# Spectral mixing plus an MLP on one Trainium2 core: a step's rounding issued ahead of the next tile, step-2 copies together on ScalarE, and the last piece of w2 prepared later

## The chip, the core and the metric

The kernel runs on one core of one Trainium2 chip. The metric is the device time of one launch in microseconds. Three runs of the kernel before gave 1115.87, 1113.58 and 1115.8 us, a median of 1115.8 us. The profile is that of one more execution of the same program.

Five engines matter. TensorE (PE in the profile, its weight loads PEld) multiplies; VectorE (DVE) and ScalarE (ACT) work on tiles in SBUF and PSUM; GpSimd (POOL) folds inputs and scatters outputs; SyncE (SP) issues transfers. Each engine executes its own instructions in the order in which the program issues them, and waits in that order.

## The reference

For each of 8 batches, x is 3136 x 256. What is computed is the real part of a two-dimensional DFT followed by a normalised MLP with a residual:

```python
X = np.fft.fft(np.fft.fft(x, axis=1), axis=2)
x = X.real
mu  = x.mean(-1, keepdims=True)
var = ((x - mu) ** 2).mean(-1, keepdims=True)
xn  = (x - mu) / np.sqrt(var + 1e-6) * g_ln
out = x + np.maximum(xn @ w_ch1, 0.0) @ w_ch2        # 256 -> 1024 -> 256
```

The last axis of the DFT is never carried out for the MLP: the kernel multiplies it, with the gain and the mean's removal, into w1 beforehand. The input is real, so rows k and N-k of the spectrum share one computation: of 3136 rows in a batch 1569 are computed, and each gives two outputs ("plus" and "minus" side).

## The kernel before, in words

**Tiles.** The 8 x 1569 tokens stand in one row, cut into 49 chunks of 256 (the last has 264). A chunk's hidden layer is cut into 8 tiles of 128 of the 1024 features. One *step* s is one such tile: chunk s // 8, feature tile s % 8. There are 392 steps. Every operand of these products is split into a high part, rounded to TensorE's fast format, and a low part, the remainder; a product takes three passes (PASSES: w_hi with the low part, w_lo with the high part, w_hi with the high part).

**A step's three functions.** `moe1_a(s)` issues 6 matmuls into a PSUM tile `ab` (L364; two such buffers), then one copy of one half on ScalarE (`asb`, L368), then the sum and the difference of the halves on VectorE (`h`, L369 and L373). `moe1_b(s)` rounds that tile: ReLU with rounding on ScalarE (`h_hi`, L380), and the remainder on VectorE (`h_lo`, L381). `moe2(s)` issues 12 matmuls that multiply h_hi and h_lo of step s with w2 into PSUM tiles `acc` (L448). In the loop (L838) step s issues moe1_a(s), then the lists described below, moe1_b(s - 1), and moe2(s - 3).

**Side work.** Two dictionaries, `late` and `after`, hold functions by step number, written out before the loop. What is in `late[s]` is issued between moe1_a(s) and moe1_b(s - 1); what is in `after[s]` comes at the end of step s. The side work has a period of 8 steps. With s0 = 8c + 5 for chunk c:

- after s0: `step2(m, "mh")`, the second DFT step for the next tokens: 8 matmuls (L318) per m into one PSUM tile, and the copy `ckh` that rounds it (ScalarE, L336). There are 61 such m in the loop for 48 chunks, so some steps have two, the second of them in the PSUM tile with the tag "y". Then `residual` for both halves of chunk c: 8 matmuls `psy` (L467).
- late s0+1: `step2(m, "fl")`: the full copy `ck` (ScalarE, L338) and the remainder `ckl` (VectorE, L340), piece by piece where m's tokens lie in two chunks; then `residual_e` (ScalarE, L474 and L475, twice).
- late s0+2 and s0+3: `residual_y` (VectorE, L481, L482, L491, L492); the second time also L496 on VectorE and the square root `ve` on ScalarE (L498), which waits for it.
- late s0+4: `inverse_std`, four short VectorE instructions (L505 to L509).
- late s0+6 and s0+7: `finish` (VectorE, L521 and L523), and after it `store_out`: an indirect DMA on GpSimd's queue (L422) and plain DMAs on SP's.

The input side of the next batch (folding on GpSimd L227, L228, L233, L234, L245; `fold_hi` on ScalarE L239; `step1`, three long matmuls L282 and a copy on ScalarE L285) is spread over 24 steps of each batch, at most two pieces per chunk: step1 falls at s0+3 and s0+6, the GpSimd subtraction L245 at s0 and s0+3.

**Prologue.** Before the loop the weights are turned from 64-bit floats into pairs of tiles. For w2 this goes in four pieces of 512 columns: `convert_a` (VectorE L571, L573; ScalarE L579), `convert_b` (VectorE L584, L586), `finish_w2` (VectorE L637), `split_w2` (ScalarE L590, then GpSimd L591). Steps 0 to 5 are written out by hand between these pieces; the piece 3 of w2 is first needed by moe2(6), in step 9.

Of the kernel before, what the change touches and what calls it, by code (L numbers as in the profile page):

```python
# [144 lines left out]
def tile_kernel(ctx: ExitStack, tc: tile.TileContext, x, g_ln, w1, w2, tu, tab, tz, ty, tw, idx, out):  # L145
# [156 lines left out]
    def width(c):  # L302
        return LASTW if c == NCH - 1 else CW
# [4 lines left out]
    def step2(m, part, of=None):  # L308

        b, j = divmod(m, 8)  # L310
        base, end = gb[2 * j], gb[2 * j + 2]
        if "m" in part:
            ps2[m] = psum.tile([128, 2, CW], F32, tag="y" if m in second else "fft", name=f"ps2_{m}")
        ps = ps2[m]
        for g in (2 * j, 2 * j + 1) if "m" in part else ():
            k0, k1 = gb[g], gb[g + 1]
            for h in range(2):
                nc.tensor.matmul(ps[:, h, k0 - base:k1 - base], s2[b][:KP, g, 128 * h:128 * h + 128],  # L318
                                 tab_s[:, h, k0:k1], start=(h == 0 and g == 2 * j), stop=True,
                                 skip_group_check=True)  # L320
            if g == 0:
                nc.tensor.matmul(ps[:, 1, 0:50], zmu, tz_s, start=False, stop=True,
                                 skip_group_check=True)
        t = b * HALF + base
        stop = b * HALF + end
        while t < stop:
            c = min(t // CW, NCH - 1)
            n = min(stop, c * CW + width(c)) - t
            if c not in chunk:
                chunk[c] = (work.tile([128, 2, MAXW], F32, tag="ck", name=f"ck{c}", bufs=3),  # L330
                            work.tile([128, 2, MAXW], F32R, tag="ck_hi", name=f"ckh{c}", bufs=3),
                            work.tile([128, 2, MAXW], F32R, tag="ck_lo", name=f"ckl{c}", bufs=3))
            full, hi, lo = (x[:, :, t - c * CW:t - c * CW + n] for x in chunk[c])
            src = ps[:, :, t - b * HALF - base:t - b * HALF - base + n]
            if "h" in part and of in (None, c):
                nc.scalar.copy(hi, src)  # L336
            if "f" in part:
                nc.scalar.copy(full, src)  # L338
            if "l" in part and of in (None, c):
                nc.vector.tensor_tensor(out=lo, in0=src, in1=hi.bitcast(F32), op=ALU.subtract)  # L340
            t += n
# [4 lines left out]
    def hcols(c):  # L346

        return 2 * CW if width(c) == CW else LASTW + 32 + CW

    def moe1_a(s, passes=((0, 1), (1, 0), (0, 0))):  # L350
        c, f = divmod(s, 8)
        w = width(c)
        ch = chunk[c][1:]
        fs = slice(128 * f, 128 * f + 128)
        wt = (w1_hi, w1_lo)
        if w <= CW:
            ab = psum.tile([128, 2, CW], F32, tag="ab", name=f"ab{s}", bufs=2)
            pa, pb = ab[:, 0], ab[:, 1]
        else:
            pa = psum.tile([128, MAXW], F32, tag="ab", name=f"aa{s}", bufs=2)  # L360
            pb = psum.tile([128, MAXW], F32, tag="fft", name=f"bb{s}")
        for j, pt in ((0, pa), (1, pb)):
            for n, (wi, xi) in enumerate(passes):
                nc.tensor.matmul(pt, wt[wi][:, j, fs], ch[xi][:, j, :w],  # L364
                                 start=(n == 0), stop=(n == 2))
        asb = work.tile([128, MAXW], F32, tag="asb", name=f"asb{s}")
        h = hh[s] = work.tile([128, hcols(c)], F32, tag="h", name=f"h{s}", bufs=4)
        nc.scalar.copy(asb[:, :w], pa)  # L368
        nc.vector.tensor_tensor(out=h[:, :w], in0=asb[:, :w], in1=pb, op=ALU.add)  # L369
        if w > CW:  # L370
            nc.vector.tensor_tensor(out=h[:, w:w + 32], in0=asb[:, w - 32:w], in1=pb[:, w - 32:w],
                                    op=ALU.subtract)
        nc.vector.tensor_tensor(out=h[:, -CW:], in0=asb[:, :CW], in1=pb[:, :CW], op=ALU.subtract)  # L373

    def moe1_b(s):
        h = hh[s]
        n = hcols(s // 8)
        h_hi = work.tile([128, n], F32R, tag="h_hi", name=f"h_hi{s}", bufs=4)
        h_lo = work.tile([128, n], F32R, tag="h_lo", name=f"h_lo{s}", bufs=4)
        nc.scalar.activation(h_hi, h, AF.Relu)  # L380
        nc.vector.scalar_tensor_tensor(out=h_lo, in0=h, scalar=0.0, in1=h_hi.bitcast(F32),  # L381
                                       op0=ALU.max, op1=ALU.subtract)
        hh[s] = (h_hi, h_lo)

    def toks(c):
        t = [(0, 0), (128, 128)]
        if width(c) > CW:
            t.append((LASTW - 32, CW))
        return t
# [39 lines left out]
    def moe2(s, tiles=(0, 1, 2)):  # L429
        c, f = divmod(s, 8)  # L430
        hs = hh[s]
        ws = (w2_hi, w2_lo)
        for i, (t0, _) in enumerate(toks(c)):
            if i not in tiles:
                continue
            if f == 0:
                acc[c, i] = psum.tile([128, 2, D], F32, tag="y" if tail(i) else f"acc{c % 2}",
                                      name=f"acc{c}_{i}", bufs=1 if tail(i) else 2)
            if tail(i):
                for n, (wi, xi) in enumerate(PASSES):  # L440
                    nc.tensor.matmul(acc[c, i][:64, 0], hs[xi][:, t0:t0 + 64], ws[wi][:, f],
                                     start=(f == 0 and n == 0), stop=(f == 7 and n == 2),
                                     skip_group_check=True)
                continue
            for side in range(2):
                h0 = t0 + side * (hcols(c) - CW)
                for n, (wi, xi) in enumerate(PASSES):
                    nc.tensor.matmul(acc[c, i][:, side], hs[xi][:, h0:h0 + 128], ws[wi][:, f],  # L448
                                     start=(f == 0 and side == 0 and n == 0),
                                     stop=(f == 7 and n == 2), skip_group_check=True)  # L450
# [130 lines left out]
    def convert_b(key):  # L581
        high, e, f = conv[key]
        e = e.bitcast(I32)
        nc.vector.tensor_scalar(out=e, in0=e, scalar1=3, scalar2=0x7F800000,  # L584
                                op0=ALU.logical_shift_left, op1=ALU.bitwise_and)
        nc.vector.scalar_tensor_tensor(out=e, in0=high, scalar=-0x80000000, in1=e,  # L586
                                       op0=ALU.bitwise_and, op1=ALU.bitwise_or)

    def split(hi, lo, src, eng=nc.vector):
        nc.scalar.copy(hi, src)  # L590
        eng.tensor_tensor(out=lo, in0=src, in1=hi.bitcast(F32), op=ALU.subtract)  # L591
# [43 lines left out]
    def finish_w2(n):  # L635
        _, e, f = conv.pop(f"w2_{n}")
        nc.vector.scalar_tensor_tensor(out=f, in0=f, scalar=2.0 ** -20, in1=e, op0=ALU.mult,  # L637
                                       op1=ALU.mult)
        return f

    def split_w2(n, f):
        split(w2_hi[:, 2 * n:2 * n + 2], w2_lo[:, 2 * n:2 * n + 2],
              f.rearrange("p (f d) -> p f d", f=2), nc.gpsimd)

    after, late = {}, {}

    def add(s, fn, *args):

        after.setdefault(s, []).append((fn, args))

    def add_late(s, fn, *args):

        late.setdefault(s, []).append((fn, args))

    first = {}
    for m in range(3, 64):
        t0 = (m // 8) * HALF + gb[2 * (m % 8)]
        s = 8 * min(t0 // CW, NCH - 1) - 3
# [2 lines left out]
        first.setdefault(s, []).append(m)  # L661
    for s, ms in first.items():
        for m in ms:
            add(s, step2, m, "mh")
        for m in ms:
            add_late(s + 1, step2, m, "fl")
    for b in range(1, NB):
        need = 8 * (b * HALF // CW) - 3
        at = [need - d for d in ((45, 42, 37, 34, 29, 26, 21) if b > 1 else
# [15 lines left out]
    for c in range(NCH):  # L685
        n = len(toks(c))
        s = 8 * c + (5 if n == 2 else 4)
        if c == 0:
            s = 6
# [20 lines left out]
    with tc.manual_schedule(engines={E.PE, E.Activation, E.DVE, E.Pool}):  # L710
        with tc.manual_schedule(engines={E.SP}):
# [84 lines left out]
            f = finish_w2(0)  # L796
# [8 lines left out]
            f = finish_w2(1)  # L805
# [18 lines left out]
            f = finish_w2(2)  # L824
            split_w2(2, f)
            moe1_a(5)
            moe1_b(4)
            step2(2, "hfl")
            moe2(2)
            convert_a("w2_3", w2p[3])  # L830
            convert_b("w2_3")
            moe1_b(5)
            f = finish_w2(3)
            split_w2(3, f)

        main.append(True)
        lag, last = 3, 8 * NCH
        for s in range(6, last):  # L838
            moe1_a(s)
            for fn, args in late.get(s, ()):  # L840
                fn(*args)
            if s > 6:
                moe1_b(s - 1)
            moe2(s - lag)
            for fn, args in after.get(s, ()):
                fn(*args)
# [25 lines left out]
```

## Time and profile before

| what | value |
|---|---|
| median of three runs | 1115.8 us (1113.58 to 1115.87) |
| the profiled execution's own time | 1114.09 us |
| its span | 1112.2 us |
| PE busy | 1045.4 us, 94% |
| DVE busy | 857.3 us, 77% |
| ACT busy | 527.7 us, 47% |
| POOL busy | 355.8 us, 32% |
| mean granted clock of PE | 0.991 |

The span runs from the first to the last instruction; the run's time is 1.9 us more. Busy shares are of the span. PE's matmuls overlap: one takes about 0.28 us by the profile, and the next starts about 0.12 us after it did. A wait is listed as "who <- whom: us in total, times, longest". The chain of waits follows the work that ended last back through whatever released it.

### The profile page before, as it was taken

The page shows a single profiled execution, that of the slowest core. Times are in us where ns is not written, and L with a number is a line of the kernel's source. Part 1 is how long each engine was busy: PE and PEld are TensorE (multiplying, and loading weights), DVE is VectorE, ACT ScalarE, POOL GpSimd, SP SyncE. Part 2 cuts the span into 40 slices and gives each one's busy share as a digit, 9 for nine tenths or more (in the row PEclk, how much of TensorE's full clock was granted, in tenths as well). Part 3 has the DMA queues.
Part 4 walks back from the last instruction along what each step waited for, and adds up shares of the span by engine and source line. Part 5 has one row for each costly group of instructions (what it writes and reads, how often), then busy time and mean ns, then how long its engine had stood idle before and what let it go on. Part 6 is the DMA issues. An engine that isn't in the chain of part 4 may idle for free.

```text
span 1112.2 us, 22526 instructions
## 1 busy us (share of the span) xinstructions
PE 1045.4 (94%) x8313; PEld 1006.2 (90%) x8314; DVE 857.3 (77%) x2200; ACT 527.7 (47%) x1398; POOL 355.8 (32%) x456
## 2 busy tenths in 40 slices
PE   7889999999999999999999999999999999999997
PEld 5589999999999999999999999999999999989986
DVE  4788877877778868887787777887788778677685
ACT  2445544454455444554455445454455544444442
POOL 2427424530445224450263323541245301001001
PEclk9989999999999999999999999999999999999999
DMA  8931631153111810155011630127002131001001
GB/s 278 257 78 55 172 107 38 59 163 96 39 39 52 218 48 24 45 142 146 20 58 39 173 105 21 39 90 206 22 29 68 39 96 38 21 20 32 28 20 41
DMA packets 44612, 90.63 MB, mean 81 GB/s; under 512 B 6984, under 2 KB 33992, under 8 KB 43608
## 3 DMA queue, kind: packets, MB, share of 16 engines
q1 hardware_dynamic: 35335, 55.33, 17.3%
q0 software_dynamic: 8192, 32.82, 10.2%
q8 instruction: 66, 1.08, 0.4%
q10 hardware_dynamic: 976, 1.05, 0.3%
q14 instruction: 43, 0.34, 0.1%
HBM read 48.74 MB, written 40.44 MB: 80 GB/s over the span
## 4 chain that ended last, share of the span: by engine, by line
PE 46%; DVE 27%; issue 13%; ACT 10%; POOL 2%; DMA 1%; SPq 0%; POOLq 0%; ACTq 0%; DVEq 0%
PE acc L448 23%; PE ab L364 12%; DVE h_lo L381 8%; PE ps L318 4%; DVE h L369 4%; ACT h_hi L380 4%; DVE h L373 4%; PE psy L467 3%; DVE st L491 3%; ACT ye L475 2%; DVE ckl L340 2%; ACT asb L368 2%; PE ps L282 1%; DVE y L482 1%; DVE y L481 1%
## 5 line engine op out<-in xcount | busy, mean ns | idle before, releaser
L448 PE MATMUL acc<-w_hi,h_lo 128*128 128x256 f32 x1568 | 453.0, 289 | 40.0 <-DVE h_lo L381 39.9
L448 PE MATMUL acc<-w_lo,h_hi 128*128 128x256 f32 x1568 | 441.3, 281 | 0.7 <-POOL w_lo L591 0.7
L448 PE MATMUL acc<-w_hi,h_hi 128*128 128x256 f32 x1568 | 440.9, 281 | 0.0
L381 DVE SCALAR_TENSOR_TENSOR h_lo<-h,h_hi 128x512 fp32r<-128x512 f32 (+1 forms) x392 | 324.7, 829 | 88.9 <-ACT h_hi L380 88.9
L448 PEld LDWEIGHTS acc<-w_hi,h_lo 128*128 128x128 f32 x1568 | 296.4, 189 | 55.8 <-DVE h_lo L381 51.6
L448 PEld LDWEIGHTS acc<-w_lo,h_hi 128*128 128x128 f32 x1568 | 296.5, 189 | 0.9 <-POOL w_lo L591 0.9
L448 PEld LDWEIGHTS acc<-w_hi,h_hi 128*128 128x128 f32 x1568 | 296.3, 189 | 0.0
L422 POOL DMA_INDIRECT out<-o,idx_s x99 | 99.5, 1005 | 589.8 <-DVE o L521 581.6
L380 ACT ACTIVATE h_hi<-h 128x512 fp32r<-128x512 f32 (+1 forms) x392 | 248.5, 634 | 9.7 <-DVE h L373 9.1
L369 DVE TENSOR_TENSOR h<-asb,ab 128x256 f32<-128x256 f32 x384 | 159.4, 415 | 103.1 <-ACT asb L368 101.6
L368 ACT COPY asb<-ab 128x256 f32<-128x256 f32 x384 | 142.4, 371 | 202.2 <-PE ab L364 196.9
L364 PE MATMUL ab<-ckl,w_hi 128*128 128x256 f32 x768 | 221.5, 288 | 4.3 <-DVE h L373 4.3
L364 PE MATMUL ab<-ckh,w_lo 128*128 128x256 f32 x768 | 217.0, 283 | 0.3 <-ACT ckh L336 0.3
L364 PE MATMUL ab<-ckh,w_hi 128*128 128x256 f32 x768 | 216.1, 281 | 0.0
L373 DVE TENSOR_TENSOR h<-asb,ab 128x256 f32<-128x256 f32 x384 | 158.4, 413 | 0.0
L364 PEld LDWEIGHTS ab<-ckl,w_hi 128*128 128x128 f32 x768 | 146.1, 190 | 7.2 <-ACT ye L474 4.3
L364 PEld LDWEIGHTS ab<-ckh,w_lo 128*128 128x128 f32 x768 | 146.5, 191 | 2.8 <-ACT ckh L336 0.5
L364 PEld LDWEIGHTS ab<-ckh,w_hi 128*128 128x128 f32 x768 | 146.1, 190 | 0.0
L245 POOL TENSOR_TENSOR fl<-f,fh 128x512 fp32r<-128x512 f32 x49 | 63.1, 1288 | 106.0 <-ACT fh L239 105.3
L498 ACT ACTIVATE ve<-ve 128x2 f32<-128x2 f32 (+1 forms) x49 | 10.1, 206 | 173.5 <-DVE ve L496 173.5
L336 ACT CAST ckh<-ps 128x392 fp32r<-128x392 f32 (+49 forms) x112 | 34.4, 349 | 75.1 <-PE ps L318 72.8
L318 PE MATMUL ps<-tab_s,s 112*128 112x98 f32 (+1 forms) x512 | 65.6, 273 | 2.5 <-issue 2.5
(122 smaller groups left out, 1070.8 us busy)
## 6 DMA issues: line engine op xcount, KB each, us to landing
scratch<-s SPq DMA_DIRECT2D x49, 256.0 KB
s<-scratch SPq DMA_DIRECT2D x7, 1792.0 KB
x<-x SPq DMA_DIRECT2D x19, 448.0 KB
out<-o SPq DMA_DIRECT2D x154, 49.0 KB
w1p_all<-w SPq DMA_DIRECT2D x8, 512.0 KB
out<-o,idx_s POOLq DMA_INDIRECT x99, 3.8
x<-x POOLq DMA_DIRECT2D x3, 448.0 KB, 16.2
x<-x SPq DMA_DIRECT2D x6, 192.0 KB
```

Of the source, the lines that this page charges most:

```text
L245: nc.gpsimd.tensor_tensor(out=lo, in0=f, in1=hi.bitcast(F32), op=ALU.subtract)
L318: nc.tensor.matmul(ps[:, h, k0 - base:k1 - base], s2[b][:KP, g, 128 * h:128 * h + 128], tab_s[:, h, k0:k1], start=(h == 0 and g == 2 * j), ...
L336: nc.scalar.copy(hi, src)
L364: nc.tensor.matmul(pt, wt[wi][:, j, fs], ch[xi][:, j, :w], start=(n == 0), stop=(n == 2))
L368: nc.scalar.copy(asb[:, :w], pa)
L369: nc.vector.tensor_tensor(out=h[:, :w], in0=asb[:, :w], in1=pb, op=ALU.add)
L373: nc.vector.tensor_tensor(out=h[:, -CW:], in0=asb[:, :CW], in1=pb[:, :CW], op=ALU.subtract)
L380: nc.scalar.activation(h_hi, h, AF.Relu)
L381: nc.vector.scalar_tensor_tensor(out=h_lo, in0=h, scalar=0.0, in1=h_hi.bitcast(F32), op0=ALU.max, op1=ALU.subtract)
L422: stored(lambda: nc.gpsimd.indirect_dma_start(out, bass.IndirectOffsetOnAxis(ap=ix, axis=0), o, None), mybir.EngineType.Pool)
L448: nc.tensor.matmul(acc[c, i][:, side], hs[xi][:, h0:h0 + 128], ws[wi][:, f], start=(f == 0 and side == 0 and n == 0), stop=(f == 7 and n = ...
L467: nc.tensor.matmul(ps[:p, j, :129 + j], ck[:, j], ty_s[:, j, :129 + j], start=(j == 0), stop=True, skip_group_check=True)
```

## The change

Three edits.

In the loop, moe1_b(s - 1) is issued first in step s, ahead of moe1_a(s); before, it stood behind moe1_a(s) and behind `late[s]`. `moe1_b(5)`, which the prologue issued, is now the first instruction group of the loop.

Of step 2, the full copy `ck` (part "f") moves from the step after into the step that issues the matmuls and the rounding copy; in the step after only the remainder `ckl` (part "l") is left. The same is done for step2(2) in the prologue, where "hfl" becomes "hf" and then "l".

The end of w2's preparation (piece 3) leaves the prologue: `convert_b` goes to late[6], and `finish_w2` with `split_w2`, as the new function `make_w2`, to late[7].

```diff
+    def make_w2(n):
+        split_w2(n, finish_w2(n))
...
         for m in ms:
-            add(s, step2, m, "mh")
+            add(s, step2, m, "mhf")
         for m in ms:
-            add_late(s + 1, step2, m, "fl")
+            add_late(s + 1, step2, m, "l")
...
-            step2(2, "hfl")
+            step2(2, "hf")
+            step2(2, "l")
             moe2(2)
             convert_a("w2_3", w2p[3])
-            convert_b("w2_3")
-            moe1_b(5)
-            f = finish_w2(3)
-            split_w2(3, f)
+            add_late(6, convert_b, "w2_3")
+            add_late(7, make_w2, 3)
...
         for s in range(6, last):
+            moe1_b(s - 1)
             moe1_a(s)
             for fn, args in late.get(s, ()):
                 fn(*args)
-            if s > 6:
-                moe1_b(s - 1)
             moe2(s - lag)
```

## The prediction

> **What bounds the kernel now.** I read the page first, then PE's waits inside the loop, then the waits of DVE and ACT, and then one period of eight steps in the chain and in the timelines. Page and PE's waits (60 to 1100 us):
>
> ```profile
> PE 1045.4 (94%) x8313; PEld 1006.2 (90%) x8314; DVE 857.3 (77%) x2200; ACT 527.7 (47%) x1398; POOL 355.8 (32%) x456
> ...
> L381 DVE SCALAR_TENSOR_TENSOR h_lo<-h,h_hi 128x512 fp32r<-128x512 f32 (+1 forms) x392 | 324.7, 829 | 88.9 <-ACT h_hi L380 88.9
> ...
> L245 POOL TENSOR_TENSOR fl<-f,fh 128x512 fp32r<-128x512 f32 x49 | 63.1, 1288 | 106.0 <-ACT fh L239 105.3
> ```
>
> ```profile
> PE acc L448 <- DVE h_lo L381: 38.3, 54, 1.0
> PE ab L364 <- DVE h L373: 4.1, 1, 4.1
> ```
>
> PE is the bound, and what it loses in the loop is one thing: moe2 waits for h_lo, 54 times, about once per chunk. Such a wait costs more than its idle time. This is one of them, in PE's timeline, and the chain around it:
>
> ```profile
> 337.06 0.28 PE L364 MATMUL ab<-ckh,w_hi 128*128 128x256 f32 x1
> 338.13 0.38 PE L448 MATMUL acc<-w_hi,h_lo 128*128 128x256 f32 x1 [0.78 <-DVE h_lo L381]
> 338.35 0.27 PE L448 MATMUL acc<-w_lo,h_hi 128*128 128x256 f32 x1
> ```
>
> ```profile
> 322.03 0.71 PE ab L364 x6
> 322.74 1.44 PE acc L448 x12
> 324.18 1.76 PE ps L318 x16
> 325.94 0.92 PE psy L467 x8
> 326.86 0.73 PE ab L364 x6
> ```
>
> Matmuls otherwise start 0.12 us apart. Start to start across the wait is 1.07 us, and 0.22 to the one behind it: 0.95 + 0.10 = 1.05 lost, 0.26 more than the idle 0.78. So 38.3 + 54 x 0.26 = **52 us** hang on h_lo. A step of PE is 0.70 to 0.71 + 1.43 to 1.44 = 2.14 us; step 2 with two m adds 1.76 (0.88 each), the residual 0.92.
>
> Why h_lo is late shows in DVE's timeline of that period (s0 = step of the 1.76 us), with ACT's:
>
> ```profile
> 329.94 0.46 DVE L340 TENSOR_TENSOR ckl<-ps,ckh 128x286 fp32r<-128x286 f32 x1 [0.47 <-ACT ck L338]
> 331.38 0.69 DVE L381 SCALAR_TENSOR_TENSOR h_lo<-h,h_hi 128x512 fp32r<-128x512 f32 x1 [0.98 <-ACT h_hi L380]
> 331.99 0.41 DVE L369 TENSOR_TENSOR h<-asb,ab 128x256 f32<-128x256 f32 x1
> 332.32 0.41 DVE L373 TENSOR_TENSOR h<-asb,ab 128x256 f32<-128x256 f32 x1
> 332.65 0.28 DVE L481 TENSOR_TENSOR y<-ye,psy 128x129 f32<-128x129 f32 x1
> ...
> 333.72 0.83 DVE L381 SCALAR_TENSOR_TENSOR h_lo<-h,h_hi 128x512 fp32r<-128x512 f32 x1
> ...
> 335.14 0.28 DVE L481 TENSOR_TENSOR y<-ye,psy 128x129 f32<-128x129 f32 x1
> ...
> 337.38 0.69 DVE L381 SCALAR_TENSOR_TENSOR h_lo<-h,h_hi 128x512 fp32r<-128x512 f32 x1 [0.79 <-ACT h_hi L380]
> ```
>
> ```profile
> 325.08 0.49 ACT L336 CAST ckh<-ps 128x392 fp32r<-128x392 f32 x1 [1.34 <-PE ps L318]
> ...
> 336.73 0.62 ACT L380 ACTIVATE h_hi<-h 128x512 fp32r<-128x512 f32 x1
> ```
>
> These h_lo belong to s0, s0+1 and s0+2. After PE's burst (step 2, residual) DVE first does h(s0+1) and the remainders, in alternation with ACT's copies, then h_lo(s0), which has waited since h(s0); every later h_lo stands behind the next tile's h and a residual. PE wants h_lo(s0+2) at 337.35 and gets it at 338.13.
>
> **The change part by part.** *Order in a step.* No instruction is added or removed. Before: h(s), late(s), h_lo(s-1). After: h_lo(s-1), h(s), late(s). Queued behind the waiting h_hi(s-1) on ACT is now asb(s), and behind h_lo(s-1) on DVE is h(s), for which PE waits two steps on, since `ab` has two buffers. So a ring appears: h_hi, h_lo, h, h, next h_hi. Its length: h_hi start to h_lo start 336.73 to 337.38 = 0.65; h_lo to h 331.38 to 331.99 = 0.61; then 0.33, then 0.41 and a hand-over, which I estimate at 0.04: **2.04 us**, under PE's 2.14. Late DVE work runs while h_hi does, so it lengthens the ring only beyond 0.70: first residual 332.65 to 333.72 = 1.07, step 0.61 + 0.66 + 1.07 = 2.34; second residual with the square root 335.14 to 337.38 = 2.24, step 3.51; remainders of two m up to about 1.0, step 2.3; inverse_std and finish about 0.7 and 0.8 (finish from L521 to the next h_lo, below: 0.78), step 2.06 at most. Eight steps: 2.04 x 3 + 2.1 + 2.34 + 3.51 + 2.06 x 2 = **18.2 us** on DVE. PE's eight: 8 x 2.14 + 61/48 x 0.88 + 0.92 = 19.2, so on average PE stays the bound.
>
> ```profile
> 321.78 0.48 DVE L521 SCALAR_TENSOR_TENSOR o<-acc,r,y 128x256 f32<-128x256 f32 x1
> 322.17 0.47 DVE L523 SCALAR_TENSOR_TENSOR o<-acc,r,y 128x256 f32<-128x256 f32 x1
> 322.56 0.69 DVE L381 SCALAR_TENSOR_TENSOR h_lo<-h,h_hi 128x512 fp32r<-128x512 f32 x1
> ```
>
> Locally I walk the same period. ACT rounds and copies the two m behind PE's 325.94 until about 327.0, then h_hi(s0) to 327.65, just as moe1_a(s0+1) ends at 327.59; h_lo(s0) to 328.3, h(s0+1) to 329.0, 1.4 after its matmuls. Remainders and h_lo(s0+1) follow, h(s0+2) at 331.0 to 331.4. First residual: h(s0+3) 0.2 later still against PE, 1.7. Second: h(s0+4) 3.51 - 2.14 = 1.4 later, **3.1 us** behind its matmuls. h_lo(s0+2) ends near 333, 4 us before PE wants it: that wait goes wholly. The one that is late next is `ab`: moe1_a(s+2) starts 30 matmuls of 0.118 after the end of moe1_a(s), less 0.28 for the modelled end, plus 0.12, so h(s) may be 3.3 us late. The margin at s0+4 is 0.2 us; where a step1 falls at s0+3, PE's extra 0.7 makes it 0.9.
>
> What eats that margin is GpSimd. DVE's and POOL's timelines:
>
> ```profile
> 323.91 2.83 DVE L381 SCALAR_TENSOR_TENSOR h_lo<-h,h_hi 128x512 fp32r<-128x512 f32 x1
> ```
>
> ```profile
> 323.54 1.29 POOL L245 TENSOR_TENSOR fl<-f,fh 128x512 fp32r<-128x512 f32 x1
> 324.77 0.73 POOL L233 TENSOR_TENSOR f<-zw 128x256 f32<-128x256 f32 x1
> 325.46 0.73 POOL L234 TENSOR_TENSOR f<-zw 128x256 f32<-128x256 f32 x1
> ```
>
> An h_lo that starts inside the folding takes 2.83 instead of 0.69. All of that, (829 - 690) ns x 392 = 54 us, lies today where DVE would wait for PE's burst anyway; in the ring it delays h. 54 us over the 49 foldings (L245) is 1.1 each; they fall on some 25 chunks, in which step1 lengthens PE by 1.4 and the slack to 19.2 + 1.4 - 18.2 = 2.4, 58 us in all. The average is covered, single hits are not. I put the remaining `ab` waits at 0.25 us a chunk, between 0 (the walk as it stands) and 0.75 (margin overrun by 0.5, with the 0.26): **+12 us**, bounds 0 and +36.
>
> The Trainium skill, "SBUF — State Buffer", section "Who interferes with whom", says that a DVE instruction with two SBUF inputs and a GpSimd one that reads SBUF exclude each other for the whole of whichever starts first. The trace agrees, but its 2.14 us of blocking spans three POOL instructions; by the page's one (1.29) the 49 foldings could take at most 63 us, and the slower rival below would shrink to about 1076.
>
> *Copies in one go.* ACT's and DVE's waits:
>
> ```profile
> ACT ck L338 <- DVE ckl L340: 41.0, 46, 0.9
> DVE ckl L340 <- ACT ck L338: 18.5, 47, 0.5
> ```
>
> Both waits go. They stand in the same stretch ahead of the late h_lo, so their worth is inside the 52, not beside it. `ck` now runs in ACT's wait for PE's burst; without that cover it would put its 0.5 us on h_hi(s0).
>
> *w2's end.* Chain, DVE, PE and POOL at the loop's start:
>
> ```profile
> 70.95 2.56 PE acc L448 x12
> ```
>
> ```profile
> 65.12 0.42 DVE L584 TENSOR_SCALAR ew<-ew 128x512 int32<-128x512 int32 x1
> 65.57 0.69 DVE L586 SCALAR_TENSOR_TENSOR ew<-w1p_all,ew 128x512 int32<-128x512 int32 x1
> 66.18 0.69 DVE L381 SCALAR_TENSOR_TENSOR h_lo<-h,h_hi 128x512 fp32r<-128x512 f32 x1
> 66.78 0.69 DVE L637 SCALAR_TENSOR_TENSOR fw<-fw,ew 128x512 f32<-128x512 f32 x1
> 68.42 0.42 DVE L369 TENSOR_TENSOR h<-asb,ab 128x256 f32<-128x256 f32 x1 [0.96 <-ACT asb L368]
> ```
>
> ```profile
> 69.32 0.55 PE L364 MATMUL ab<-ckl,w_hi 128*128 128x256 f32 x1 [4.08 <-DVE h L373]
> ```
>
> ```profile
> 68.20 1.27 POOL L591 TENSOR_TENSOR w_lo<-fw,w_hi 128x512 fp32r<-128x512 f32 x1 [5.85 <-ACT w_hi L590]
> ```
>
> h(6) stands behind convert_b (65.12 to 66.18) and, through ACT's copy of w2, behind fw; PE waits 4.08 us for it and then runs at half pace (2.56 for 1.43; the matmuls of both steps behind the wait lose some 2 us). After the change h_lo(5) starts 1.06 earlier and another 0.5 for the copies of step2(2), near 64.6, and h(6), next in the queue, runs from 65.2 to 65.9, 3.3 us ahead of today's 69.2. Given back: DVE then has convert_b 1.06, h_lo(6) 0.6, h(7) 0.66 and fw 0.6 to 68.8, ACT some 0.6, POOL 1.27: w_lo at 70.7. PE is at moe2(6) near 69.0 (65.9 + 0.71 + 1.43, a wait for h(7) until 68.2, 0.71) and waits 1.7; I allow 0.6 for what DVE's later steps lose. Net 3.3 + 2 - 1.7 - 0.6 = **-3 us**, from 0 (the half pace comes back at the new wait) to -5 (no loss in the later steps, w_lo in time).
>
> Sum from the execution's 1114.1: - 52 + 12 - 3 = **1071 us**. That execution lies 1.7 under the median and inside the runs' spread, so I add nothing.
>
> **The rivals.** *Nothing is left over* (the margin always holds): 1114 - 52 - 5 = 1057. For it: the walk. Against it: the margin of 0.2. *The wait moves to `ab` nearly in full*: 0.75 a chunk, +36: 1114 - 52 + 36 - 3 = 1095. For it: hand-overs of 0.1 more in three ring steps use up the margin. *The reorder doesn't reach the stall*, because the square root still holds h_hi back (0.79 idle stays): 1113. Against it: h_lo(s0+2) has 4 us to spare. *Slower*: every folding blocks a ring h_lo for the full 2.14: 49 x 2.14 = 105 against 58 of slack, 47 us: 1114 - 52 + 12 - 3 + 47 = 1118. It decides from (52 - 12 + 3 + 58) / 49 = 2.06 us per folding; the average today is 1.1.
>
> **How the numbers follow.** Forecast (1062 to 1085) 0.55, nothing left 0.12, wait moved 0.20, no effect 0.05, slower 0.08. Three runs spread over 0.2%, so less than that counts as the same: faster 0.87, same 0.05, slower 0.08. 1058 to 1096 leaves the last two and a little at the low end outside.
>
> **What would show it.** Right: PE's waits for h_lo fall from 54 to a few, none near 1 us; the waits between ck and ckl vanish; a wait of `ab` on h appears with some 5 to 20 us in total, at s0+4; the 4.08 us at the loop's start become under 2 and a wait for w_lo appears; DVE waits more for h_hi (88.9 us now) since the ring exposes it. Wrong: waits for h_lo stay near 38 us, or `ab` on h passes 40 us with long h_lo next to POOL's folding.

## The result and the profile after

The changed kernel takes 1058.2 us (median of four runs, 1057.27 to 1058.92) against 1115.8 us on the same chip: a ratio of 0.9485, with a 95% interval of 0.9466 to 0.9503. That is 57.6 us less. The forecast was 1071, the range 1058 to 1096; the time lies at the range's lower edge, where the rival "nothing is left over" (1057) stood.

The page after the change, engines and the groups that answer to those shown before (columns: busy us, mean ns of one, idle before and what ended it):

```profile
PE 1027.1 (97%) x8314; PEld 999.4 (95%) x8314; DVE 824.7 (78%) x2200; ACT 533.9 (51%) x1398; POOL 364.7 (35%) x456
...
L448 PE MATMUL acc<-w_hi,h_lo 128*128 128x256 f32 x1568 | 441.3, 281 | 1.1 <-DVE h_lo L381 0.9
...
L381 DVE SCALAR_TENSOR_TENSOR h_lo<-h,h_hi 128x512 fp32r<-128x512 f32 (+1 forms) x392 | 295.4, 754 | 182.9 <-ACT h_hi L380 180.1
```

PE's waits after the change, 60 to 1100 us (us in total, times, longest):

```profile
PE ab L364 <- DVE ve L505: 2.6, 2, 1.5
PE pse L257 <- DVE ckl L340: 2.3, 2, 1.2
...
PE ab L364 <- DVE h L373: 1.2, 2, 0.7
...
PE acc L448 <- POOL w_lo L591: 1.0, 1, 1.0
PE acc L448 <- DVE h_lo L381: 0.7, 1, 0.7
```

The wait for h_lo, 38.3 us in 54 times before, is one wait of 0.7, and that one stands at 1045 us, behind the loop; inside the loop there is none. The waits between ck and ckl are gone. DVE waits twice as long for h_hi as before (180 us against 88.9): the ring is there, and it costs nothing, since PE doesn't wait for it. Engines by stretch, before and after (length of the window, then busy us of PE, PEld, DVE, ACT and POOL, PE's granted clock, the DMAs' share and GB/s):

```profile
200.00:300.00 100.00, 95.53 (x779) 93.14 (x778) 78.45 (x210) 49.24 (x132) 29.68 (x39) 1.00 0.31 89
900.00:1000.00 100.00, 94.59 (x781) 92.43 (x781) 73.70 (x207) 45.06 (x125) 11.17 (x20) 1.00 0.14 42
```

```profile
200.00:300.00 100.00, 99.85 (x834) 98.84 (x833) 80.17 (x217) 52.56 (x141) 36.34 (x44) 1.00 0.33 94
900.00:1000.00 100.00, 100.00 (x854) 100.00 (x854) 80.31 (x225) 51.38 (x140) 11.14 (x22) 1.00 0.10 31
```

PE is busy throughout at full clock: inside the loop hardly any wait is left to be won.

The period that the prediction walked through comes 8.95 us earlier now (its residual starts at 316.82 instead of 325.77). ACT and DVE in it:

```profile
316.12 0.49 ACT L336 CAST ckh<-ps 128x392 fp32r<-128x392 f32 x1 [1.25 <-PE ps L318]
316.51 0.49 ACT L338 COPY ck<-ps 128x392 f32<-128x392 f32 x1
...
317.59 0.43 ACT L338 COPY ck<-ps 128x286 f32<-128x286 f32 x1
317.88 0.67 ACT L380 ACTIVATE h_hi<-h 128x512 fp32r<-128x512 f32 x1
```

```profile
318.58 0.98 DVE L381 SCALAR_TENSOR_TENSOR h_lo<-h,h_hi 128x512 fp32r<-128x512 f32 x1 [2.45 <-ACT h_hi L380]
319.48 0.41 DVE L369 TENSOR_TENSOR h<-asb,ab 128x256 f32<-128x256 f32 x1
319.81 0.41 DVE L373 TENSOR_TENSOR h<-asb,ab 128x256 f32<-128x256 f32 x1
320.14 1.09 DVE L340 TENSOR_TENSOR ckl<-ps,ckh 128x392 fp32r<-128x392 f32 x3
321.16 0.68 DVE L381 SCALAR_TENSOR_TENSOR h_lo<-h,h_hi 128x512 fp32r<-128x512 f32 x1
...
322.09 0.41 DVE L373 TENSOR_TENSOR h<-asb,ab 128x256 f32<-128x256 f32 x1
...
329.65 0.69 DVE L381 SCALAR_TENSOR_TENSOR h_lo<-h,h_hi 128x512 fp32r<-128x512 f32 x1
...
331.70 0.69 DVE L381 SCALAR_TENSOR_TENSOR h_lo<-h,h_hi 128x512 fp32r<-128x512 f32 x1 [0.70 <-ACT h_hi L380]
```

All copies of step 2 are on ACT in one go behind PE's burst; the remainders (three, L340) follow without a pause. h(s0+1) ends at 320.2 and h(s0+2) at 322.5; the walk, moved by 8.95, had 320.1 and 322.5. Two h_lo of steps without long late work are 329.65 to 331.70 = 2.05 us apart; the ring was put at 2.04.

**A landmark inside the loop.** The first residual starts anywhere between 61.0 and 68.0 us in the traces of this study: the prologue ahead of it, in which hardly any of the edits acts, takes longer in one execution than in another. So beside whole times I compare the stretch from the fourth residual (chunk 3) to that of chunk 47, both starts in PE's timeline, here before and after:

```profile
131.37 1.08 PE L467 MATMUL psy<-ty_s,ck 128*128 128x129 f32 x8
1070.55 1.08 PE L467 MATMUL psy<-ty_s,ck 128*128 128x129 f32 x8
```

```profile
132.93 1.08 PE L467 MATMUL psy<-ty_s,ck 128*128 128x129 f32 x8
1015.30 1.08 PE L467 MATMUL psy<-ty_s,ck 128*128 128x129 f32 x8
```

939.2 us before, 882.4 after: 56.8 us, practically the whole gain, lie there. Some 1.5 us of it are no work of the change: in the execution before, PE ran at about half its clock (granted clock 0.51) from 179.8 to 183.3 us; that of the kernel with w2's edit alone, where it didn't, takes 937.7 us for the same stretch.

### The profile page after: what moved, and what is told of

Read it like the earlier page. It is cut to its first block, busy times and chain, and to the rows that moved or that the text cites. A ratio compares the mean times of both kernels' runs of the same rounds, so it can differ in the third digit from the quotient of the medians.

```text
span 1056.3 us, 22463 instructions
## 1 busy us (share of the span) xinstructions
PE 1027.1 (97%) x8314; PEld 999.4 (95%) x8314; DVE 824.7 (78%) x2200; ACT 533.9 (51%) x1398; POOL 364.7 (35%) x456
## 4 chain that ended last, share of the span: by engine, by line
PE 56%; DVE 19%; issue 14%; ACT 7%; POOL 2%; DMA 1%; SPq 0%; POOLq 0%; DVEq 0%; ACTq 0%
PE acc L448 30%; PE ab L364 16%; DVE h_lo L381 7%; PE ps L318 4%; ACT h_hi L380 4%; DVE h L369 3%; DVE h L373 3%; PE psy L467 2%; PE ps L282 2%; DVE st L491 1%; POOL out L422 1%; DMA x<-x 1%; ACT ckh L336 1%; ACT s L285 1%; PE ps L275 1%
## 5 line engine op out<-in xcount | busy, mean ns | idle before, releaser
L448 PE MATMUL acc<-w_hi,h_lo 128*128 128x256 f32 x1568 | 441.3, 281 | 1.1 <-DVE h_lo L381 0.9
L381 DVE SCALAR_TENSOR_TENSOR h_lo<-h,h_hi 128x512 fp32r<-128x512 f32 (+1 forms) x392 | 295.4, 754 | 182.9 <-ACT h_hi L380 180.1
L422 POOL DMA_INDIRECT out<-o,idx_s x99 | 102.4, 1034 | 580.5 <-DVE o L521 572.3
L364 PE MATMUL ab<-ckl,w_hi 128*128 128x256 f32 x768 | 222.1, 289 | 5.5 <-DVE ve L505 2.6
L364 PE MATMUL ab<-ckh,w_lo 128*128 128x256 f32 x768 | 215.8, 281 | 0.3 <-ACT ckh L336 0.3
L364 PE MATMUL ab<-ckh,w_hi 128*128 128x256 f32 x768 | 215.1, 280 | 0.0
L373 DVE TENSOR_TENSOR h<-asb,ab 128x256 f32<-128x256 f32 x384 | 158.1, 412 | 0.0
L364 PEld LDWEIGHTS ab<-ckl,w_hi 128*128 128x128 f32 x768 | 144.5, 188 | 11.1 <-issue 7.0
L368 ACT COPY asb<-ab 128x256 f32<-128x256 f32 x384 | 138.6, 361 | 18.2 <-PE ab L364 15.6
L364 PEld LDWEIGHTS ab<-ckh,w_lo 128*128 128x128 f32 x768 | 145.0, 189 | 2.8 <-ACT ckh L336 0.5
L364 PEld LDWEIGHTS ab<-ckh,w_hi 128*128 128x128 f32 x768 | 144.8, 188 | 0.0
L245 POOL TENSOR_TENSOR fl<-f,fh 128x512 fp32r<-128x512 f32 x49 | 63.5, 1295 | 46.7 <-ACT fh L239 45.9
L336 ACT CAST ckh<-ps 128x392 fp32r<-128x392 f32 (+49 forms) x112 | 39.5, 355 | 54.6 <-PE ps L318 33.0
```

The lines of the kernel that those rows point to most:

```text
L245: nc.gpsimd.tensor_tensor(out=lo, in0=f, in1=hi.bitcast(F32), op=ALU.subtract)
L364: nc.tensor.matmul(pt, wt[wi][:, j, fs], ch[xi][:, j, :w], start=(n == 0), stop=(n == 2))
L422: stored(lambda: nc.gpsimd.indirect_dma_start(out, bass.IndirectOffsetOnAxis(ap=ix, axis=0), o, None), mybir.EngineType.Pool)
```

## The experiments

### One part at a time

The three edits were made alone, and the first two together.

```diff
 # the order alone
+            if s > 6:
+                moe1_b(s - 1)
             moe1_a(s)
             for fn, args in late.get(s, ()):
                 fn(*args)
-            if s > 6:
-                moe1_b(s - 1)
```

> The kernel before with only the loop's order changed (moe1_b(s-1) first). Theory: the order alone takes the wait of moe2 for h_lo away, whatever the copies do: that wait under 3 us in PE's list, time 50 to 56 us under the kernel before; the alternation of ck and ckl is still there (some 40 and 18 us) and now delays h(s0+2), so a wait of ab on h of 0 to 5 us is left. Rival (the parts add up): the copies carry a good part, the order alone gives only 25 to 40 us.

1106.9 us, ratio 0.9907 (0.9892 to 0.9922); the stretch 929.6, of which some 3 are lost at half clock near 184 and 822 us. Only 9 us: theory and rival both fall. PE's waits (60 to 1045 us; up to 1100 it is 38.0 us in 43 times), ACT's, and one place in DVE's and PE's timelines:

```profile
PE ab L364 <- DVE ve L505: 37.3, 42, 1.4
```

```profile
ACT ck L338 <- DVE ckl L340: 45.8, 46, 1.7
```

```profile
936.54 0.41 DVE L369 TENSOR_TENSOR h<-asb,ab 128x256 f32<-128x256 f32 x1
936.87 0.41 DVE L373 TENSOR_TENSOR h<-asb,ab 128x256 f32<-128x256 f32 x1
```

```profile
937.43 0.36 PE L364 MATMUL ab<-ckl,w_hi 128*128 128x256 f32 x1 [0.68 <-DVE ve L505]
```

The wait for h_lo has gone, and one of the same size has come for `ab`, once a chunk. The listing names L505, the instruction started last; what PE's buffer needs is h(s0+4), which ends at 936.87 + 0.41 = 937.28, 0.15 before PE starts. The alternation of ck and ckl now stands ahead of h(s0+2): by the ends of L364 and L373 in 41 chunks, h(s0+2) is done 2.7 us behind its matmuls instead of 1.5 in the changed kernel, and h(s0+4) 4.2 instead of 3.1.

```diff
 # the copies alone
-            add(s, step2, m, "mh")
+            add(s, step2, m, "mhf")
-            add_late(s + 1, step2, m, "fl")
+            add_late(s + 1, step2, m, "l")
-            step2(2, "hfl")
+            step2(2, "hf")
+            step2(2, "l")
```

> The kernel before with only step 2's copies together on ACT. Theory: they shorten the queue ahead of the late h_lo by 1.3 to 1.8 us per chunk (walked through the same period: h_lo(s0) from 331.4 to about 329.8, h_lo(s0+2) from 337.4 to about 335.6, wanted by PE near 336.8), which is more than the wait of about 1.05 us; so this edit alone too takes 35 to 52 us, and the two edits overlap almost fully. Rival, the prediction as it was written would allow it: the copies' waits are cover only, the edit alone gives under 15 us.

1059.9 us, ratio 0.9495 (0.9478 to 0.9512); the stretch 885.4. PE's waits (60 to 1100 us):

```profile
PE ab L364 <- DVE h L373: 3.2, 1, 3.2
PE acc L448 <- DVE h_lo L381: 2.6, 5, 1.4
```

The copies alone bring nearly everything (56 us; the theory had 35 to 52).

```diff
 # w2's end alone
-            convert_b("w2_3")
             moe1_b(5)
-            f = finish_w2(3)
-            split_w2(3, f)
+            add_late(6, convert_b, "w2_3")
+            add_late(7, make_w2, 3)
```

> The kernel before with only the end of w2 spread (convert_b in late[6], finish and split in late[7]; moe1_b(5) stays where it was). Theory: the 4.08 us wait of ab near 65 us falls under 2.5 us and the half pace behind it goes, a wait for w_lo of 0 to 2 us appears: 2 to 5 us less in all. Rival: what is won at 69 us is given back at steps 7 to 9, no change (within 2 us).

1114.2 us, ratio 0.9977 (0.9966 to 0.9989): 2.1 us, at the foot of the theory's range. PE at the loop's start:

```profile
70.91 0.36 PE L364 MATMUL ab<-ckl,w_hi 128*128 128x256 f32 x1 [0.85 <-DVE h L373]
75.69 0.39 PE L448 MATMUL acc<-w_hi,h_lo 128*128 128x256 f32 x1 [1.72 <-DVE h_lo L381]
81.60 0.35 PE L448 MATMUL acc<-w_hi,h_lo 128*128 128x256 f32 x1 [1.13 <-DVE h_lo L381]
```

The 4.08 became 0.85; two waits for h_lo follow, the given-back part (the expected wait for w_lo doesn't show here).

The order and the copies together, without w2's edit:

> The changed kernel without the spreading of w2. Theory: order and copies together give 53 to 57 us under the kernel before, the 4.08 us wait near 65 us shrinks to 1 to 3 us because h(6) no longer stands behind late work, so w2's spreading is worth 0 to 3 us. Rival: the wait stays at 4 us with the half pace behind it, and this is 5 or more us slower than the changed kernel.

1057.9 us, ratio 0.9476 (0.9461 to 0.9490), 58.5 us less where the theory had 53 to 57; the stretch 882.2. The loop's start in PE's timeline, and the chain there:

```profile
67.90 0.55 PE L364 MATMUL ab<-ckl,w_hi 128*128 128x256 f32 x1 [3.26 <-DVE h L373]
```

```profile
69.52 2.17 PE acc L448 x12
71.69 0.70 PE ab L364 x6
```

A wait of 3.26 us stays, with some of the half pace behind it (2.17 for 1.43). The wait is between theory and rival, and yet the whole time is that of the changed kernel. Between the first and the fourth residual this kernel takes 68.4 us, the changed one 68.2 and, in a second execution, 67.2.

So the parts don't add up: 9 (order) + 56 (copies) + 2 (w2) would be 67. Either of the first two moves work out of one and the same queue. The order alone puts h_lo ahead and h behind, and the wait moves; only the shorter queue takes it away.

### Which half of the copies' edit

Here all of ck is copied, then all of ckl computed, but still in the step after:

```diff
-            add_late(s + 1, step2, m, "fl")
+            add_late(s + 1, step2, m, "f")
+        for m in ms:
+            add_late(s + 1, step2, m, "l")
```

> The kernel before, but in the step after step 2 all of ck is copied first and then all of ckl computed: no alternation between ACT and DVE, the copies still behind asb(s0+1). It splits what the copies' edit does in two. Theory: both halves count. The alternation is worth some 0.8 us of the 1.6 us by which h_lo(s0) comes earlier, the cover of PE's burst the other 0.8; the wait of 0.7 us idle per chunk nearly goes: 30 to 48 us under the kernel before, some short waits for h_lo left (under 15 us in all). Rival A (the alternation is everything): 52 us or more, as with the whole edit. Rival B (the place is everything): under 20 us.

1071.3 us, ratio 0.9615 (0.9578 to 0.9652), 45 us less; the stretch 897.8. PE's wait (60 to 1100 us; the longest of these lies behind the loop):

```profile
PE acc L448 <- DVE h_lo L381: 12.1, 26, 1.4
```

As the theory had it: without the alternation of the two engines over one PSUM tile 45 of 56 us are there; the place under PE's burst brings the other 11.

### How much room is left

Two instructions of 0.42 us each by the profile were added on VectorE in every chunk but the first and the last; they read a constant table, and nothing reads their result. First in step s0+3, in the changed kernel and in that with the copies alone, then in step s0.

```diff
+    def more():
+        for _ in range(2):
+            nc.vector.bn_stats(out=junk, in_=tab_s[:, 0, :256])
+
+    for c in range(1, NCH - 1):
+        add_late(8 * c + 5 + 3, more)
```

> The changed kernel with 0.92 us of VectorE work added in each chunk ahead of the first instruction late in step s0+3 (two statistics instructions over a constant table whose result nothing reads). Theory: h(s0+4) has 0.38 us of slack on average before moe1_a(s0+6) wants its buffer (least 0.14), so PE now waits for it some 0.5 us in nearly every chunk, with 0.2 of restart: 22 to 42 us more than the changed kernel, as a wait of ab on DVE, none for h_lo. Rival (the ring is elastic over the chunk, the added work goes into later slack): under 10 us.

> The same 0.92 us added at the same place to the kernel with only the copies together (old order). Theory: there h_lo(s0+2) has only 0.14 us of slack, so PE waits for h_lo some 0.8 us per chunk: 38 to 52 us more than without the added work, as a wait for h_lo. So the new order would leave a little more room than the old one at this place, though both cost the same now. Rival: the old order lets h(s) through first and loses less than the new one, under 25 us.

> The changed kernel with the same 0.92 us added in step s0 instead, where DVE waits for ACT's copies, which wait for PE's burst. Theory: the burst hides it, 0 to 3 us more than the changed kernel, and no new wait on PE. Rival (DVE has no room anywhere in the chunk, its ring sets the time): 20 us or more.

1086.8 us (28.6 more than the changed kernel, theory), 1091.6 us (31.7 more than the copies alone, between theory and rival), and 1057.2 us (no more than the changed kernel, theory). PE's waits of the first, the second and the third (60 to 1045 us):

```profile
PE ab L364 <- DVE ve L505: 21.3, 32, 2.3
```

```profile
PE acc L448 <- DVE h_lo L381: 26.4, 41, 0.9
```

```profile
PE ab L364 <- DVE ve L505: 2.6, 2, 1.5
```

By the traces the two instructions put off VectorE's next one by 0.80 us, not 0.92: from the start of h (L373) to that of L481 it is 1.13 us with them and 0.33 without. These 0.80 us cost 0.6 to 0.7 us a chunk at s0+3 and nothing at s0. The two orders have their narrowest place behind the same work, the second residual of s0+3, the new one at `ab`, the old one at h_lo. Those slacks include the hand-over: no step, however late, showed less than 0.14 between h and PE, or 0.05 between h_lo and PE, so the real room is on average 0.24 us (0.38 - 0.14) with the new order and 0.09 (0.14 - 0.05) with the old. What is left of the 0.80, 0.56 and 0.71 us, is near the measured 0.61 and 0.67 a chunk. That 0.80 were added and not 0.92 is a part of why the second kernel lost 32 and not the expected 38 to 52; the rest stays open.

### The one place where the ring still breaks

In the changed kernel's trace, DVE, POOL and PE near 93 us, where the second batch's folding is denser than elsewhere:

```profile
93.16 3.33 DVE L381 SCALAR_TENSOR_TENSOR h_lo<-h,h_hi 128x512 fp32r<-128x512 f32 x1
```

```profile
91.97 1.29 POOL L245 TENSOR_TENSOR fl<-f,fh 128x512 fp32r<-128x512 f32 x1
93.23 0.73 POOL L233 TENSOR_TENSOR f<-zw 128x256 f32<-128x256 f32 x1
...
95.30 0.63 POOL L228 TENSOR_TENSOR zw<-x,x 128x256 f32<-128x256 f32 x1
```

```profile
101.20 0.36 PE L364 MATMUL ab<-ckl,w_hi 128*128 128x256 f32 x1 [1.55 <-DVE ve L505]
```

An h_lo takes 3.33 us behind five GpSimd instructions in a row, and PE waits for `ab` two steps on, at 97.3 (0.49 us) and 101.2. This is the mechanism of the slower rival, in one place. The folding of that batch was spaced otherwise:

```diff
-                                 (29, 26, 23, 21, 18, 15, 13))]
+                                 (29, 26, 21, 18, 15, 13, 11))]
```

> The changed kernel with the second batch's folding spaced otherwise, (29, 26, 21, 18, 15, 13, 11) steps ahead of its use instead of (29, 26, 23, 21, 18, 15, 13), so that GpSimd has a pause where one h_lo took 3.33 us at 93.16 us. Theory (GpSimd's block of that h_lo is what made PE wait for ab at 97.3 and 101.2): the long h_lo goes, both waits go or fall under 0.3 us, 1 to 3 us less than the changed kernel. Rival: the block moves to another h_lo of that stretch or the next chunk, no difference.

> The same spacing of the second batch's folding with order and copies, w2's end left in the prologue. Theory: like the changed kernel with that spacing within 2 us, since w2's spreading moves a wait from the loop's start to moe2(6) and gains nothing. Rival: w2's spreading is worth 2 or more us, as it was with the old order (2.1 us).

1056.4 us (ratio 0.9473, 0.9450 to 0.9495) and 1053.4 us (0.9444, 0.9421 to 0.9467), beside these two on the same chip:

> The changed kernel once more, on the same chip as the kernel with the copies alone: 1057 to 1059 us.

> The kernel before with only step 2's copies together, once more beside the changed kernel. Theory: the copies alone leave h_lo(s0+2) 0.14 us of slack, so PE hardly waits, and the order adds nothing: within 2 us of the changed kernel. Rival: the order is worth 2 to 5 us (the first comparison had 1059.9 against 1057.9 with the order).

1058.3 us (0.9474, 0.9451 to 0.9497) and 1060.3 us (0.9504, 0.9483 to 0.9524). With the new spacing the first 130 us of the loop have no h_lo over 1.4 us, and neither of the two waits. From the first residual to chunk 47 it is 946.3 us with w2's edit and 948.4 without, against 950.5 and 949.3 in the two traces of the changed kernel: 1 to 4 us. In whole times the intervals overlap, so a version that beats the changed kernel is likely, but not settled. Nor is w2's edit settled beside that spacing: the kernel without it is 3.0 us faster in whole times, more than its theory allowed, and 2.1 slower between these landmarks, 1.5 of them in a stretch at half clock near 176 us.

The order, beside the copies, is 2 us in whole times, with overlapping intervals; in the stretch from chunk 3 to 47 it is 882.1 to 882.4 against 885.4 and 885.5, some 3 us, in which the two traces of each agree within 0.3. Before chunk 3 it gives back about 2 (68.2 and 67.2 us against 65.9 and 65.8), where the broken ring of the second batch lies. From the first residual to chunk 47 that leaves 0.6 to 2.1 us (949.3 to 950.6 in the three traces with order and copies, against 951.2 and 951.3 with the copies alone).

## Why the prediction was right or wrong

**PE waits for h_lo, and that goes: right.** The wait fell from 38.3 us to none inside the loop. Its price held too, though the 0.26 us beside the idle time came from one sample. Between the landmarks of chunks 3 and 47 PE's timelines before and after hold the same 7327 instructions in the same sequence. Compared start by start, 51.1 of the 56.8 us lie at the 52 waits for h_lo there: 37.2 us idle, and 0.27 us more at each. Of the rest, 1.5 us lie in the stretch at half clock, 0.9 at two waits of another product (`pse`), and some 3 in delays of about 0.1 us, most of them at matmuls that read h_lo and those behind them.

**The ring of 2.04 us and the walk: right**, to about 0.1 us in the walked period. h(s0+4) was put 3.1 us behind its matmuls; the mean over 41 chunks is 3.08 (2.52 to 3.52).

**The remaining `ab` waits, +12 us: mis-sized.** They are 3.8 us in all (2.6 + 1.2), none of them later than 101.2 us; 12 - 3.8 = 8 of the 13 us between forecast and result are this term. What failed is the step from 1.1 us of blocking per folding: h_lo's blocked time fell to (754 - 690) ns x 392 = 25 us from 54. I took today's blocking over into a new arrangement in time. The pages of the runs with one edit show which edit does it. The copies alone, then the order alone:

```profile
L381 DVE SCALAR_TENSOR_TENSOR h_lo<-h,h_hi 128x512 fp32r<-128x512 f32 (+1 forms) x392 | 327.0, 835 | 43.9 <-ACT h_hi L380 39.4
```

```profile
L381 DVE SCALAR_TENSOR_TENSOR h_lo<-h,h_hi 128x512 fp32r<-128x512 f32 (+1 forms) x392 | 293.1, 748 | 197.4 <-ACT h_hi L380 195.8
```

With the copies alone the blocking stays at (835 - 690) ns x 392 = 57 us, and at 1059.9 us hardly costs anything; with the order alone it is 23. The order moves h_lo away from L245: h_lo starts while an L245 runs in 40 steps of the kernel before, in 15 with the order alone and in 8 of the changed kernel.

**Where the gain comes from: wrong.** The prediction gave the 52 us to the order, under "Order in a step", and let the copies' worth lie "inside the 52". The runs show the reverse: the copies alone give 56 us, the order alone 9, and beside the copies about 2. That the total came out inside the range is in part luck: it needed the copies, to which the prediction gave no worth of their own; the order alone takes 1106.9 us. The failing step is the walk: it put h(s0+2) at 331.0 to 331.4 with the copies already moved, and was read as the price of the order. Walked with one edit at a time it would have shown that the order without the copies ends at the rival "the wait moves to `ab` nearly in full"; that rival had the right mechanism, and it was the copies that held it off.

**Copies in one go.** "They stand in the same stretch ahead of the late h_lo" was right, and was the main thing.

**w2's end, -3 us:** 2.1 us alone, nothing that can be measured beside the others. The new wait for w_lo came, 1.0 us where 1.7 was expected.

**The slower rival:** its mechanism is real, at 93 us in the second batch, and rare: no h_lo behind 105 us takes over 1.3 us, and it would have to be over 2 in every folding.

## What to carry to other kernels

When several edits shorten one queue, walk the path with each of them alone before giving any of them a price: two may each be thought sufficient while one of them only moves the wait to the next buffer. Two engines that read one PSUM tile piece by piece in turns, with waits of 0.4 us on the one side and 0.9 on the other, can cost the whole chain behind them. And time a loop between two landmarks inside it, when the loads before it scatter by microseconds.

## What the hardware showed that was not expected

A wait of PE costs more than the idle time listed: 51.1 us for 52 waits of 37.2 us in all, 0.27 us more at each.

An h_lo on VectorE that starts behind a GpSimd instruction can stay blocked through several in a row: 2.83 us behind three, 3.33 behind five, where 0.69 is its own time. The Trainium skill, "SBUF — State Buffer", section "Who interferes with whom", has whichever starts first hold the shared ports for its whole instruction; the trace agrees that they exclude each other, but the block outlasted that one instruction (1.29 us), and the first to start isn't always the one that holds: eight h_lo of the kernel before that start 0.3 us ahead of an L245 take 2.14 to 2.17 us all the same.

In the loop PE's half pace followed idle times of 4.08 and 3.26 us, but it also began 1.6 us behind one of 1.60 us (178.27 us in the kernel before). It did not follow 3.24 us (69.39 us with the copies alone), 1.72 us (75.69 us with w2's edit alone), or the same 1.60 us in that kernel (181.27 us): there the matmuls soon started 0.12 us apart as ever. So the length of the idle time alone doesn't decide it in these traces, and what does stays open.
